# Attention and a two-layer feed-forward on one core: earlier due times for blocks a, b, d and VectorE's combinations in the second stage

## The chip, the cores and the metric

The kernel runs on one core of a Trainium2 chip. The time is the device time of one execution in microseconds (us); the time before is the median of three runs, 1447.98 us (1443.79 to 1448.81). The engines are called PE (matrix products; its weight loads are PEld), DVE (VectorE), ACT (ScalarE), POOL (GpSimd) and SP, which here only issues transfers.

## The reference

```python
def _attn_ref(q, k, v, g_q, g_k):            # (8, 12, 448, 64): 8 batches, 12 heads
    q_n, k_n = rmsnorm(q, g_q), rmsnorm(k, g_k)
    scores = (1 / np.sqrt(64)) * np.matmul(q_n, k_n.transpose(0, 1, 3, 2))
    attn = exp(scores - max);  attn = attn / (sum + 1e-9)
    return np.matmul(attn, v)

def _moe_ref(x, w_in, w_out):                # x: (3584, 768), w_in: (768, 2048), w_out: (2048, 768)
    h = x @ w_in
    g = h * np.cos(h)
    return g @ w_out
```

The attention's output, heads side by side, is `x`. All inputs and the output are float32.

## The kernel before, in words

The program has two stages, each with a planner of its own. The first stage does the attention of all 8 batches and the product with `w_in` for batches 0 to 6, and stores `h` in DRAM. It also makes seven combinations of quarters of `w_out` (the scheme that multiplies 2 by 2 blocks with seven products instead of eight) and stores them. The change touches the second stage alone.

The second stage begins with the product with `w_in` for batch 7 (16 blocks on PE), and then takes the batches in four pairs, 0 to 3. For each pair `h` is a matrix of 2 by 2 parts: two halves of the 2048 inner rows, two batches. The parts are called roles: a and c belong to the pair's first batch (first and second half), b and d to its second batch (likewise). Each role has four blocks, 0 to 3, of 2 x 128 rows by 448 columns, in tiles called B, so that `B1b3` is block 3 of role b of pair 1. The numbers in a profile are left out: there it is `B1b`.

A block is made so (`block`): SP loads it from DRAM (tile hb, L596); for each half ACT writes the rounded number of turns (n, L601), DVE subtracts the turns in two steps (L611 twice); ACT takes the absolute value (L615) and the sine (c, L619), and DVE multiplies c by hb (L623). There are three buffers for hb, and one each for n and c.

Seven products per pair follow on PE, called product 0 to 6. Their left operands are: a; b, after `b = d - b`; a, after `a = a + b`; c; b, after `b = d - a`; a, after `a = c - a`; and d. These combinations are written over the tiles block by block (L626). The first three run on DVE, in that order, and `a = c - a` on POOL. Before a block is multiplied, ACT casts it to a high part (ghi, L635) and POOL subtracts that from the block to get the low part (glo, L633). Both have three buffers. A product takes 4 blocks x 2 rows x 3 output columns x 3 matmuls (L648 high, L649 low, L650 with the weights' low part), 72 in all, 18 for each block. Results leave the six PSUM banks through ACT's copies (L673) and DVE's sums (L676), and go out through SP (L680). SP also loads the combined weights (wo, L279, eight buffers from product 2 on).

The order of the work on each engine is the planner's. Each piece has an engine, a cost, the pieces it depends on and a due time. The planner simulates the engines in time: whenever an engine is free, it takes, of the pieces that are ready by its own costs, the one that is due first. What comes out is one fixed list for each engine, and on the chip each engine runs its list in order, waiting where an operand is late. Due times so decide only what goes first among pieces that the planner holds ready; they delay nothing. A block's due time is given by its product's start in the planner's time (`D`), less `ahead`: the load is due 30 before that, the turns 20, the multiplication 12.

The tiles set limits of their own. Role a of the next pair takes over the tiles of c of this pair, d of the next pair those of a, and b those of b. So a block of the next pair can be begun only when the splits of its tile's last user are done.

Of the kernel before, what the change touches and what calls it, by code (L numbers as in the profile page):

```python
# [14 lines left out]
ALU = mybir.AluOpType  # L15
# [12 lines left out]
class Plan:  # L28
# [18 lines left out]
    def add(self, eng, cost, due, fn, *args, r=(), w=(), land=0.0, start=0.0, lead=None):  # L47
        n = len(self.parts)
        deps = set()
        for key in r:  # L50
            deps.update(self.writer.get(key, ()))
        for key in w:
            deps.update(self.writer.get(key, ()))
            deps.update(self.readers.get(key, ()))
        for key in (*r, *w):
            name, inst = key[0], key[1]
            if name in self.rings:
                self.users.setdefault((name, inst), []).append(n)
        for key in r:
            self.readers.setdefault(key, []).append(n)  # L60
        for key in w:
            self.writer[key] = [n]
            self.readers[key] = []
        deps.discard(n)
        self.parts.append((eng, cost, due, fn, args, deps, land))
        self.start.append(start)
        self.lead.append(self.LEAD * (eng == PE) if lead is None else lead)
# [59 lines left out]
def tile_attention_moe(  # L127
# [13 lines left out]
    B, S, D = 8, kT.shape[2], 64  # L141
# [101 lines left out]
    mix = {}  # L243
# [668 lines left out]
    for fc in range(NFC):  # L912
        d = BLOCK * fc
# [10 lines left out]
    def block(pr, role, g, d):  # L924
        i, j = ROLES[role]
        n = next(count)
        hb, B_ = ("hb", n), ("B", home(pr, role), g)
        r = [("hd", 2 * pr + j, NH * i + NG * g + f) for f in range(NG)]
        add(SP, ISS, d - 30.0, gl_load, pr, role, g, r=r, w=[hb], land=LAND)
        for f in range(NG):  # L930
            t = ("n", NG * n + f)
            add(ACT, 0.56, d - 20.0 + 1.5 * f, g_turns, pr, role, g, f, r=[hb], w=[t])
            add(DVE, 0.63, d - 19.0 + 1.5 * f, g_reduce, pr, role, g, f, 0, r=[hb, t], w=[B_])
            add(DVE, 0.63, d - 18.5 + 1.5 * f, g_reduce, pr, role, g, f, 1, r=[t], w=[B_])
        add(ACT, 0.96, d - 15.0, g_abs, pr, role, g, w=[B_])
        for f in range(NG):
            c = ("c", NG * n + f)
            add(ACT, 0.57, d - 13.0 + 1.5 * f, g_cos, pr, role, g, f, r=[B_], w=[c])
            add(DVE, 0.63, d - 12.0 + 1.5 * f, g_mul, pr, role, g, f, r=[hb, c], w=[(*B_, f)])

    def block_keys(pr, role, g):
        B_ = ("B", home(pr, role), g)
        return [B_] + [(*B_, f) for f in range(NG)]

    def mix(pr, to, a, c, op, d, eng=DVE):
        e, cost = (nc.vector, 1.2) if eng == DVE else (nc.gpsimd, 2.3)
        for g in range(NGR):
            add(eng, cost, d + BLOCK * g, g_mix, pr, to, a, c, g, op, e,
                r=sum((block_keys(pr, x, g) for x in (a, c) if x != to), []), w=block_keys(pr, to, g))

    def product(pr, pi, role):
        d0 = T0 + PROD * (NPR * pr + pi)
        for kk in range(NH // 2):
            if pi >= 2 or pr == 0:
                s = slot(pr, pi, kk)
                add(SP, ISS, d0 + BLOCK * kk - 24.0, v_place, pr, pi, kk, s, w=[("w", s)], land=8.0)
        for k in range(NH):
            d = d0 + PART * k
            g = k // NG
            if k % NG == 0:  # L960
                n = next(split_n)
                Bs, hi, lo = block_keys(pr, role, g), ("ghi", n), ("glo", n)
                add(ACT, 0.96, d - 8.0, g_split, pr, pi, role, g, 0, r=Bs, w=[hi])
                add(POOL, 2.3, d - 6.0, g_split, pr, pi, role, g, 1, r=Bs + [hi], w=[lo])
            s = slot(pr, pi, k // 2)
            add(PE, PART, d, ffn2, pr, pi, k, s, r=[hi, lo, ("w", s)], w=[("y", bank(pr, pi, oc)) for oc in range(NO)])
        return d0 + PROD

    def copies(pr, pi, name, d, where=None):
        for oc in range(NO):  # L970
            y = ("y", bank(pr, pi, oc))
            if where and pr == NPAIR - 1 and oc == NO - 1:
                add(ACT, 0.3, d + oc, e_copy, pr, pi, oc, name, 0, r=[y], w=[(name, oc)])
                add(DVE, 0.35, d + oc, e_copy, pr, pi, oc, name, 1, r=[y], w=[(name, oc, 1)])
            else:
                add(ACT, 0.53, d + oc, e_copy, pr, pi, oc, name, r=[y], w=[(name, oc)])
            if where:
                add(SP, ISS, d + oc + 1, e_store, pr, oc, name, *where, r=[(name, oc), (name, oc, 1)], land=LAND)

    def sums(pr, pi, to, a, d, where=None):  # L980
        for oc in range(NO):
            add(DVE, 0.63, d + oc, e_add, pr, pi, oc, to, a,
                r=[("y", bank(pr, pi, oc))] + ([(a, oc)] if a != to else []), w=[(to, oc)])
            if where:
                add(SP, ISS, d + oc + 1, e_store, pr, oc, to, *where, r=[(to, oc)], land=LAND)

    for pr in range(NPAIR):
        D = [T0 + PROD * (NPR * pr + pi) for pi in range(NPR + 1)]
        for roles, pi, ahead in (("a", 0, 12.0), ("bd", 1, 18.0), ("c", 3, 12.0)):
            for g in range(NGR):  # L990
                for n, role in enumerate(roles):
                    block(pr, role, g, D[pi] + BLOCK * g - ahead + 2 * n)
        d = product(pr, 0, "a")
        mix(pr, "b", "d", "b", ALU.subtract, D[1] - 12.0)
        copies(pr, 0, "e1", d + 1)
        mix(pr, "a", "b", "a", ALU.add, D[2] - 14.0)
        d = product(pr, 1, "b")
        copies(pr, 1, "e7", d + 1)
        d = product(pr, 2, "a")
        mix(pr, "b", "d", "a", ALU.subtract, D[3] - 10.0)  # L1000
        sums(pr, 2, "u3", "e7", d + 1)
        mix(pr, "a", "c", "a", ALU.subtract, D[3] - 2.0, POOL)
        d = product(pr, 3, "c")
        sums(pr, 3, "e1", "e1", d + 1, (0, 0))
        d = product(pr, 4, "b")
        sums(pr, 4, "c22", "e7", d + 1, (1, 1))
        d = product(pr, 5, "a")
        sums(pr, 5, "u3", "u3", d + 1, (1, 0))
        d = product(pr, 6, "d")
        copies(pr, 6, "c12", d + 1, (0, 1))  # L1010
# [52 lines left out]
```

## Time and profile before

| | before |
|---|---|
| median of three runs | 1447.98 us (1443.79 to 1448.81) |
| the profiled execution's own time | 1448.93 us |
| its span, first to last instruction | 1447.1 us |
| PE busy | 1397.0 us, 97% |
| PEld busy | 1152.7 us, 80% |
| DVE, ACT, POOL busy | 1020.8, 1001.6 and 932.6 us |
| mean granted PE clock | 0.998 |

Times inside a profile are counted from the span's start. In the answers that are quoted below, a row of a timeline has the start, the duration, the engine, the line, the operation, what is written and read, the number of instructions merged in it, and in brackets how long the engine sat idle before it and what ended that. A row of a table of stretches has the stretch, its length, the busy time and number of instructions of PE, PEld, DVE, ACT and POOL, the granted PE clock, the share of the DMA engines and the GB/s. Rows of waits have the total, the number of times and the longest.

### The profile page before, as it was taken

How to read it: one execution, taken by the hardware profiler on the slowest of the kernel's cores; microseconds unless marked ns; L12 is line 12 of the kernel's file. 1: busy time of each engine (PE TensorE's matmuls, PEld its weight loads, DVE VectorE, ACT ScalarE, POOL GpSimd, SP SyncE). 2: the span in 40 equal slices, each digit the busy share in tenths (PEclk: the TensorE clock that was granted, in tenths of full speed). 3: DMA queues.
4: the chain of work that ended last, by engine and by line, in shares of the span. 5: the costliest groups of instructions: out<-in, count | busy, mean ns of one | idle time of the engine just before them, and what ended most of it. 6: DMA issues, size and time to landing. Idle time of an engine off the chain costs nothing.

```text
span 1447.1 us, 22426 instructions
## 1 busy us (share of the span) xinstructions
PE 1397.0 (97%) x7361; PEld 1152.7 (80%) x7361; DVE 1020.8 (71%) x1649; ACT 1001.6 (69%) x2058; POOL 932.6 (64%) x722
## 2 busy tenths in 40 slices
PE   6999999999999999999999999999999999999998
PEld 2445687888888788787878788889889899899898
DVE  6878885677778777869676755536876876977821
ACT  5777677677777777777776676547676776786742
POOL 5678777566877867787884673101295596585684
PEclk9999999999999999999999999999999999999999
DMA  6788444555667576566654542149569569489373
GB/s 207 230 259 255 129 129 133 151 175 173 192 200 222 166 219 206 185 206 188 215 184 159 163 149 87 55 132 347 195 201 327 188 224 338 154 265 339 124 238 101
DMA packets 154452, 282.62 MB, mean 195 GB/s; under 512 B 31760, under 2 KB 102368, under 8 KB 154336
## 3 DMA queue, kind: packets, MB, share of 16 engines
q1 hardware_dynamic: 154336, 281.20, 60.7%
q8 instruction: 58, 0.95, 0.3%
q14 instruction: 58, 0.48, 0.1%
HBM read 218.24 MB, written 62.89 MB: 194 GB/s over the span
## 4 chain that ended last, share of the span: by engine, by line
PE 71%; DVE 14%; ACT 5%; DMA 4%; issue 4%; POOL 2%; SPq 0%; ACTq 0%; DVEq 0%; POOLq 0%
PE ph L573 9%; PE PT L483 8%; PE ph L574 8%; PE ph L575 8%; PE O L514 8%; PE S L438 7%; PE y L649 7%; PE y L650 7%; PE y L648 7%; DVE lo L502 2%; DMA hb<-h_d 2%; ACT hi L494 1%; POOL glo L633 1%; DVE sm L447 1%; PE O L522 1%
## 5 line engine op out<-in xcount | busy, mean ns | idle before, releaser
L573 PE MATMUL ph<-xs,wi 128*128 128x448 f32 x768 | 299.2, 390 | 1.5 <-ACT he L585 1.5
L574 PE MATMUL ph<-xs,wi 128*128 128x448 f32 x768 | 281.1, 366 | 0.0
L575 PE MATMUL ph<-xs,wi 128*128 128x448 f32 x768 | 281.0, 366 | 0.0
L456 ACT ACTIVATE P<-S,sm 128x448 f32<-128x448 f32 x336 | 213.7, 640 | 78.7 <-DVE sm L447 66.6
L649 PE MATMUL y<-glo,wo 128*128 128x448 f32 x672 | 247.1, 368 | 7.3 <-POOL glo L633 7.3
L648 PE MATMUL y<-ghi,wo 128*128 128x448 f32 x672 | 246.8, 367 | 0.3 <-ACT ghi L635 0.3
L650 PE MATMUL y<-ghi,wo 128*128 128x448 f32 x672 | 246.7, 367 | 0.0
L494 ACT CAST hi<-PT 128x448 fp32r<-128x448 f32 x312 | 153.5, 536 | 93.9 <-PE PT L483 49.6
L447 DVE TENSOR_REDUCE sm<-S 128x1 f32<-128x448 f32 x322 | 186.7, 611 | 25.6 <-PE S L438 24.9
L483 PEld LDWEIGHTS PT<-ident,P 128*128 128x128 f32 x1344 | 155.5, 141 | 41.6 <-issue 22.8
L502 DVE TENSOR_TENSOR lo<-PT,hi 128x448 fp32r<-128x448 f32 x234 | 134.7, 617 | 71.5 <-ACT hi L494 70.2
L483 PE MATMUL PT<-ident,P 128*128 128x128 f32 x1344 | 181.2, 275 | 3.0 <-DVE hi L492 3.0
L573 PEld LDWEIGHTS ph<-xs,wi 128*128 128x128 f32 x768 | 144.5, 188 | 34.9 <-issue 15.7
L575 PEld LDWEIGHTS ph<-xs,wi 128*128 128x128 f32 x768 | 144.2, 188 | 12.6
L574 PEld LDWEIGHTS ph<-xs,wi 128*128 128x128 f32 x768 | 144.9, 189 | 9.7 <-issue 0.4
L649 PEld LDWEIGHTS y<-glo,wo 128*128 128x128 f32 x672 | 126.6, 188 | 19.4 <-POOL glo L633 8.7
L306 POOL TENSOR_TENSOR r<-r,nhalf 128x14 f32<-128x14 f32 (+1 forms) x50 | 128.5, 2570 | 12.5 <-DVE r L324 8.9
L648 PEld LDWEIGHTS y<-ghi,wo 128*128 128x128 f32 x672 | 126.6, 188 | 11.7 <-ACT ghi L635 0.7
L650 PEld LDWEIGHTS y<-ghi,wo 128*128 128x128 f32 x672 | 126.6, 188 | 10.9
L438 PE MATMUL S<-khi,qhi 64*128 64x448 f32 x399 | 115.0, 518 | 1.7 <-ACT khi L343 1.2
L514 PE MATMUL O<-hi,vs 128*128 128x448 f32 x312 | 101.9, 381 | 7.3 <-ACT hi L494 3.3
L514 PE MATMUL O<-lo,vs 128*128 128x448 f32 x234 | 89.3, 397 | 10.3 <-DVE lo L502 9.8
(225 smaller groups left out, 2710.7 us busy)
## 6 DMA issues: line engine op xcount, KB each, us to landing
wo<-wo_d SPq DMA_DIRECT2D x88, 768.0 KB
h_d<-he SPq DMA_DIRECT2D x128, 224.0 KB
hb<-h_d SPq DMA_DIRECT2D x64, 448.0 KB
wo_d<-wv SPq DMA_DIRECT2D x56, 384.0 KB
sd<-sd SPq DMA_DIRECT2D x46, 448.0 KB
vd<-v SPq DMA_DIRECT2D x78, 160.0 KB
qd<-qT SPq DMA_DIRECT2D x48, 256.0 KB
raw<-w_in SPq DMA_DIRECT2D x16, 768.0 KB
```

Source lines behind the costliest of these rows:

```text
L438: nc.tensor.matmul(d["S", t][:, :S], d[a][p0:p1, j * 128 : j * 128 + 128], d[c][p0:p1, :], start=(n == 0), stop=(n == len(ops) - 1),)
L447: nc.vector.tensor_reduce(least, d["S", t][:, :S], axis=AX.X, op=ALU.min)
L456: nc.scalar.activation(tl(u, f"P{t}", [128, S], F32, "P"), d.pop(("S", t))[:, :S], AF.Exp, bias=sm[:, 1, t : t + 1], scale=-1.0, accum_out ...
L483: nc.tensor.transpose(pt[:, t * 128 : t * 128 + 128], src, ident)
L494: nc.scalar.copy(hi, pt[:, hh * S : hh * S + S])
L514: nc.tensor.matmul(O, st, d.pop((what, kb, hh)), start=(kc + n == 0), stop=(kc + n == 4))
L573: nc.tensor.matmul(ph[:, :S], whi, x2[:, 0, :], start=(cc == 0), stop=False)
L574: nc.tensor.matmul(ph[:, :S], whi, x2[:, 1, :], start=False, stop=False)
L575: nc.tensor.matmul(ph[:, :S], wlo, x2[:, 0, :], start=False, stop=(cc == NCC - 1))
L648: nc.tensor.matmul(y, whi, hi, start=(k == 0 and chain < 2), stop=False, skip_group_check=chain == 2)
L649: nc.tensor.matmul(y, whi, lo, start=False, stop=False, skip_group_check=chain == 2)
L650: nc.tensor.matmul(y, wlo, hi, start=False, stop=(k == NH - 1), skip_group_check=chain == 2)
```

## The change

Five due times of the second stage are set further ahead. The blocks of role a are due 30 instead of 12 ahead of their product, those of b and d 44 instead of 18; `b = d - b` 28 instead of 12, `a = a + b` 30 instead of 14, `b = d - a` 20 instead of 10. Block c, `a = c - a` on POOL, the splits, the products, the copies and sums and the weights' loads keep their due times. No instruction is added or removed; the compute engines run the same work in another order. On SP the same transfers are issued in another order too.

```diff
-        for roles, pi, ahead in (("a", 0, 12.0), ("bd", 1, 18.0), ("c", 3, 12.0)):
+        for roles, pi, ahead in (("a", 0, 30.0), ("bd", 1, 44.0), ("c", 3, 12.0)):
...
-        mix(pr, "b", "d", "b", ALU.subtract, D[1] - 12.0)
+        mix(pr, "b", "d", "b", ALU.subtract, D[1] - 28.0)
...
-        mix(pr, "a", "b", "a", ALU.add, D[2] - 14.0)
+        mix(pr, "a", "b", "a", ALU.add, D[2] - 30.0)
...
-        mix(pr, "b", "d", "a", ALU.subtract, D[3] - 10.0)
+        mix(pr, "b", "d", "a", ALU.subtract, D[3] - 20.0)
```

PE's list is the same in both kernels. On the other engines the lists differ at these three places.

First, DVE where product 1 of pair 0 needs its last block. `B0b3` and `B0a3` are block 3 of roles b and a of pair 0, `B0c0` is block 0 of role c. Before:

```order
L626 TENSOR_TENSOR B0b3_12013<-B0d3_12079,B0b3_12013 128x896
L611 SCALAR_TENSOR_TENSOR B0c0_12149<-n0c01_12157,hb0_4_12063 128x448
L611 SCALAR_TENSOR_TENSOR B0c0_12149<-n0c01_12157,B0c0_12149 128x448
L626 TENSOR_TENSOR B0a3_11624<-B0b3_12013,B0a3_11624 128x896
L626 TENSOR_TENSOR B0b2_11913<-B0d2_11972,B0a2_11558 128x896
```

Now:

```order
L626 TENSOR_TENSOR B0b3_12013<-B0d3_12079,B0b3_12013 128x896
L626 TENSOR_TENSOR B0a3_11624<-B0b3_12013,B0a3_11624 128x896
L611 SCALAR_TENSOR_TENSOR B0c0_12149<-n0c01_12157,hb0_4_12063 128x448
L611 SCALAR_TENSOR_TENSOR B0c0_12149<-n0c01_12157,B0c0_12149 128x448
L626 TENSOR_TENSOR B0b2_11913<-B0d2_11972,B0a2_11558 128x896
```

The combination of `B0a3` has moved ahead of two reductions of block c. It is the only move in pair 0 up to the end of product 2.

Second, DVE at the same place of pair 1 (pair 2 is alike). Rows of L626 that write a tile of b from d and a are `b = d - a`, for product 4. Before:

```order
L626 TENSOR_TENSOR B1b0_12627<-B1d0_12682,B1a0_12386 128x896
L626 TENSOR_TENSOR B1b1_12738<-B1d1_12843,B1a1_12457 128x896
L623 TENSOR_TENSOR B1d3_13091<-c1d30_13145,hb3_7_13022 128x448
L611 SCALAR_TENSOR_TENSOR B1c0_13163<-n1c00_13147,hb2_4_13075 128x448
L611 SCALAR_TENSOR_TENSOR B1c0_13163<-n1c00_13147,B1c0_13163 128x448
L623 TENSOR_TENSOR B1d3_13091<-c1d31_13165,hb3_7_13022 128x448
L626 TENSOR_TENSOR B1b3_13036<-B1d3_13091,B1b3_13036 128x896
```

Now:

```order
L626 TENSOR_TENSOR B1b3_12981<-B1d3_13042,B1b3_12981 128x896
L626 TENSOR_TENSOR B1a3_12573<-B1b3_12981,B1a3_12573 128x896
L611 SCALAR_TENSOR_TENSOR B1c0_13099<-n1c01_13116,hb2_4_13027 128x448
L611 SCALAR_TENSOR_TENSOR B1c0_13099<-n1c01_13116,B1c0_13099 128x448
L626 TENSOR_TENSOR B1b0_12627<-B1d0_12681,B1a0_12386 128x896
L611 SCALAR_TENSOR_TENSOR B1c1_13168<-n1c10_13165,hb2_5_13092 128x448
L611 SCALAR_TENSOR_TENSOR B1c1_13168<-n1c10_13165,B1c1_13168 128x448
L626 TENSOR_TENSOR B1b1_12741<-B1d1_12800,B1a1_12457 128x896
L626 TENSOR_TENSOR B1b2_12856<-B1d2_12915,B1a2_12498 128x896
```

The two combinations for product 4 that stood ahead of `B1b3` stand behind it now, among the reductions of block c. Two more reductions (`B1c1`, second half), the first multiplication of `B1c0`, the combination that writes `B1b3` for product 4 and two reductions of `B1c2` follow, and then the second multiplication of `B1c0`. In pair 3 only one of the two combinations has moved behind, and the second multiplication of `B3c0` comes four rows sooner than that.

Third, POOL at the turn from product 1 to product 2 of pair 1 (`glo1pk` is the low part of block k for product p). Before:

```order
L633 TENSOR_TENSOR glo113_13199<-B1b3_13036,ghi113_13193 128x896
L633 TENSOR_TENSOR glo120_13214<-B1a0_12386,ghi120_13196 128x896
L633 TENSOR_TENSOR glo121_13247<-B1a1_12457,ghi121_13229 128x896
L626 TENSOR_TENSOR B1a0_12386<-B1c0_13163,B1a0_12386 128x896
L633 TENSOR_TENSOR glo122_13286<-B1a2_12498,ghi122_13260 128x896
```

Now:

```order
L633 TENSOR_TENSOR glo113_13187<-B1b3_12981,ghi113_13183 128x896
L633 TENSOR_TENSOR glo120_13218<-B1a0_12386,ghi120_13212 128x896
L626 TENSOR_TENSOR B1a0_12386<-B1c0_13099,B1a0_12386 128x896
L633 TENSOR_TENSOR glo121_13267<-B1a1_12457,ghi121_13247 128x896
L633 TENSOR_TENSOR glo122_13287<-B1a2_12498,ghi122_13280 128x896
```

POOL's combination `a = c - a` of block 0, which reads `B1c0`, now stands ahead of the split of block 1 for product 2. It is so in pairs 1, 2 and 3, not in pair 0. On SP the last load of b and d of a pair (`hb3_7` in pair 1) has moved from behind the weights `wo1_3_3` and three stores to just behind `wo1_3_2`; in pair 3 it has only passed the three stores.

## The prediction

> **What bounds the kernel now.** I read the page first, then PE's waits in the second stage, then the timelines of the engines that PE waits for.
>
> ```profile
> span 1447.1 us, 22426 instructions
> PE 1397.0 (97%) x7361; PEld 1152.7 (80%) x7361; DVE 1020.8 (71%) x1649; ACT 1001.6 (69%) x2058; POOL 932.6 (64%) x722
> ```
>
> PE is busy for 97% of the span, and the change gives it no instruction less. So only PE's waits can be won, and only those of the second stage. From 962 us to the end these are all:
>
> ```profile
> PE y L649 <- POOL glo L633: 7.3, 4, 2.6
> PE y L648 <- ACT ghi L635: 0.3, 1, 0.3
> ```
>
> Four waits for a low part, one in each pair, and a short one for a high part. In PE's timeline they are (the first three rows are pair 0's, the next three pair 1's):
>
> ```profile
> 1047.36 0.37 PE L650 MATMUL y<-ghi,wo 128*128 128x448 f32 x1
> 1048.08 0.47 PE L648 MATMUL y<-ghi,wo 128*128 128x448 f32 x1 [0.35 <-ACT ghi L635]
> 1051.16 0.47 PE L649 MATMUL y<-glo,wo 128*128 128x448 f32 x1 [2.61 <-POOL glo L633]
> ...
> 1156.73 0.37 PE L648 MATMUL y<-ghi,wo 128*128 128x448 f32 x1
> 1158.50 0.47 PE L649 MATMUL y<-glo,wo 128*128 128x448 f32 x1 [1.41 <-POOL glo L633]
> 1158.81 0.37 PE L650 MATMUL y<-ghi,wo 128*128 128x448 f32 x1
> ...
> 1262.54 0.47 PE L649 MATMUL y<-glo,wo 128*128 128x448 f32 x1 [1.62 <-POOL glo L633]
> ...
> 1366.58 0.48 PE L649 MATMUL y<-glo,wo 128*128 128x448 f32 x1 [1.63 <-POOL glo L633]
> ```
>
> Each stands at the second matmul of block 3 of product 1: `b = d - b` is late there. The first cost more than its wait, as the table of stretches shows:
>
> ```profile
> 1051.67:1055.08 3.41, 3.41 (x11) 3.05 (x10) 3.38 (x6) 1.22 (x3) 3.41 (x2) 0.50 0.00 0
> 1158.50:1162.05 3.55, 3.55 (x17) 3.30 (x18) 3.52 (x5) 1.73 (x3) 3.55 (x2) 1.00 0.00 0
> ...
> 1115.88:1130.76 14.88, 14.88 (x74) 13.51 (x73) 10.85 (x18) 9.16 (x13) 8.00 (x5) 1.00 0.96 318
> 1191.30:1205.90 14.60, 14.60 (x74) 13.53 (x73) 9.78 (x18) 10.96 (x17) 8.07 (x4) 1.00 0.96 332
> ```
>
> After 2.61 us of idling PE was granted half its clock for 3.41 us, which loses 1.7 us; after 1.41 us (second row) nothing was taken. The last two rows show a second thing: the same work, 74 matmuls begun, takes 14.88 us before the wait at 1158.50 (in the ninth of the 28 products) and 14.60 after it. I see no cause for this spacing that the change touches, so it enters the range only.
>
> **Term 1, pair 0.** Here DVE and POOL meet:
>
> ```profile
> 1045.88 1.09 DVE L626 TENSOR_TENSOR B0b<-B0d,B0b 128x896 f32<-128x896 f32 x1
> ...
> 1048.09 1.08 DVE L626 TENSOR_TENSOR B0a<-B0b,B0a 128x896 f32<-128x896 f32 x1
> 1049.09 2.97 DVE L626 TENSOR_TENSOR B0b<-B0d,B0a 128x896 f32<-128x896 f32 x1
> ```
>
> ```profile
> 1048.10 3.00 POOL L633 TENSOR_TENSOR glo<-B0b,ghi 128x896 fp32r<-128x896 f32 x1 [5.46 <-ACT ghi L635]
> ...
> 1146.85 2.13 POOL L633 TENSOR_TENSOR glo<-B1b,ghi 128x896 fp32r<-128x896 f32 x1 [1.59 <-ACT ghi L635]
> 1155.44 3.00 POOL L633 TENSOR_TENSOR glo<-B1b,ghi 128x896 fp32r<-128x896 f32 x1 [6.47 <-ACT ghi L635]
> 1158.41 5.92 POOL L633 TENSOR_TENSOR glo<-B1a,ghi 128x896 fp32r<-128x896 f32 x2
> 1164.29 2.14 POOL L626 TENSOR_TENSOR B1a<-B1c,B1a 128x896 f32<-128x896 f32 x1
> ```
>
> A split takes 2.13 us alone, but 3.00 when DVE began a combination 0.01 us before it; the next combination then takes 2.97 instead of 1.09. One waits until the other is through. In pair 0 the combination of `B0b3` (1045.88) keeps its place, so the block itself comes no sooner. But the one of `B0a3` now follows it directly and is over at about 1048.1, when the split starts. The split ends some 0.8 us sooner, PE idles 1.8 instead of 2.6. Of the idle times shown, 1.41 to 1.63 left the clock alone (the later products ran at 14.60) and 2.61 did not; 1.8 is nearest to the former, so I count the 1.7 too. **Term 1: -2.5 us**, bounds 0 (the split is held after all) and -2.5. The rest of that wait stays.
>
> The Trainium skill ("TensorE: Matmul & The Clock Gate", "Why this matters for your kernels") asks for no idle gaps over about 3 us, as one idle window brings the half clock; here 2.61 us did, so the measurement decides. By that figure 1.8 us would be safe, and the sum the same.
>
> **Term 2, the old wait in pairs 1 to 3.** From 1156.73 to 1158.50 and 1158.81 PE made two steps in 2.08 us that take 0.41 at the spacing around them: 1.67 lost. With the idle times 1.62 and 1.63 in place of 1.41 the other two are 1.9 each: 5.5 together. What makes `B1b3` late:
>
> ```profile
> 1147.31 3.61 DVE L626 TENSOR_TENSOR B1b<-B1d,B1a 128x896 f32<-128x896 f32 x2
> 1150.85 0.61 DVE L623 TENSOR_TENSOR B1d<-c1d,hb 128x448 f32<-128x448 f32 x1
> ...
> 1153.22 1.09 DVE L626 TENSOR_TENSOR B1b<-B1d,B1b 128x896 f32<-128x896 f32 x1
> 1154.22 0.62 DVE L611 SCALAR_TENSOR_TENSOR B1c<-n1c,hb 128x448 f32<-128x448 int32 x1
> ...
> 1155.42 1.08 DVE L626 TENSOR_TENSOR B1a<-B1b,B1a 128x896 f32<-128x896 f32 x1
> 1156.42 2.98 DVE L626 TENSOR_TENSOR B1b<-B1d,B1a 128x896 f32<-128x896 f32 x1
> ...
> 1161.04 1.30 DVE L626 TENSOR_TENSOR B1b<-B1d,B1a 128x896 f32<-128x896 f32 x1
> ...
> 1163.45 0.61 DVE L623 TENSOR_TENSOR B1c<-c1c,hb 128x448 f32<-128x448 f32 x1
> ```
>
> ```profile
> 1123.44 4.08 SPq L279 DMA_DIRECT2D wo<-wo_d  x2
> 1127.61 0.42 SPq L596 DMA_DIRECT2D hb<-h_d  x1
> 1130.88 0.36 SPq L279 DMA_DIRECT2D wo<-wo_d  x1
> 1133.38 1.32 SPq L680 DMA_DIRECT2D out<-es  x3
> 1134.82 29.63 SPq L596 DMA_DIRECT2D hb<-h_d  x5
> ```
>
> Two combinations for product 4 held DVE for 3.61 us ahead of it; they have moved behind. And its last load went out at 1134.82, behind a weight at 1130.88 that waits for PE and three stores. It now stands behind the weight that goes out at about 1127.2 (the second of the merged row at 1123.44), so it can leave at 1127.7, 7.1 us sooner, in pairs 1 and 2; in pair 3, where it passes the stores only, at 1131.3, 3.5 sooner. The combination of b3 then starts between 1149.6 (3.6 sooner, by DVE's list alone) and some 1145.4 (load and list together, as far as ACT and POOL let it). I carry the load's gain through: 1146.1 in pairs 1 and 2, 1149.7 in pair 3. (I count pair 3 in pair 1's times.) The split must be done by 1156.9, where PE would go on without a wait (one place of 0.2 after 1156.73), and in between lie the combination (1.09), a cast of 0.95 and a split of 2.13 to 3.00: 2 us are to spare in pair 3 and more in the others. Only ACT's new list, which has some turns and an absolute value of block c ahead of that cast, can leave a rest: 0 to 0.8, taken as 0.2 each. **Term 2: -4.9 us**, bounds -5.5 and -3.1.
>
> **Term 3, a new wait.** On POOL `a = c - a` of block 0 now stands ahead of the split of block 1 for product 2, and so that split, which PE wants, is queued behind DVE's second multiplication of `B1c0` (1163.45 before). PE wants it two blocks after the second matmul of product 1's block 3, at 1156.9 + 2 x 3.72 (a quarter of 14.88) = 1164.4. From the combination of b3 to that multiplication DVE's new list has 6 combinations at 1.0 (1153.22 to 1154.22), 8 reductions at 0.6 (two from 1154.22 to 1155.42) and 2 multiplications at 0.6: 12.0 us. Meanwhile POOL has four splits, and combinations wait for them: in the same stretch of before, with as many of both, the rows 3.61, 1.09, 1.08, 2.98 and 1.30 are 4.1 us over six times 1.0. So `B1c0` is done at 1146.1 + 12.0 + 4.1 = 1162.2, the combination (2.14) and the split (2.13) take until 1166.5, and PE waits **2.1 us in pairs 1 and 2**. In pair 3 there are 4 combinations, 6 reductions and 2 multiplications, 8.8 us, and two thirds of the waiting, 2.7: 1149.7 + 8.8 + 2.7 + 4.3 = 1165.5, **1.1 us**. At 2.1 PE idles about 1.9, and the clock stays as in term 1. **Term 3: +5.3 us**; bounds: 0, if the combinations meet no split (1146.1 + 12.0 + 4.3 = 1162.4, in time), and 2.3 more in each pair, with a half clock's 1.7, if three whole splits are waited for (6.4 instead of 4.1; the fourth runs beside reductions). I take the value that before's own rows give.
>
> The Trainium skill ("SBUF — State Buffer", "SBUF: two separate sides") calls the pair of ports that DVE and GpSimd share an exclusive lock, held for a whole instruction; the rows 3.00 and 2.97 agree. As an estimate from that rule at its worst, four splits of 2.13 cost DVE 8.5 us instead of 4.1, the new waits would be 4 to 6.5 us, and the sum about +15.
>
> What else moves costs nothing by the cover it has: the blocks of the next pair stand earlier in ACT's list among the casts of products 5, 6 and 0, but casts wait for PE to free a buffer:
>
> ```profile
> ACT ghi L635 <- PE y L650: 71.6, 55, 2.7
> ```
>
> Such a cast (0.95) and split (2.13) end 3.1 us after the buffer is free, and PE wants them two blocks, 7.4 us, after that: 4 us of cover. Without it each microsecond more would show as a wait for glo at product 0. DVE's sums (L676) of product 5 stand a few rows later; their bank is wanted only a product later.
>
> **Sum:** 1448.9 (the profiled execution's own time) - 2.5 - 4.9 + 5.3 = **1446.8**. That execution lies 0.9 above the median of the runs, within their spread, so I leave it so.
>
> **Rivals.** *No new wait.* If block c is done in time, the whole old wait is won: 1448.9 - 2.5 - 5.5 = 1440.9. For it speaks that blocks c could start sooner too; against it, that `B1c0` has to be done at 1160.1, 4.0 sooner than in before, though two more reductions and two more combinations stand between it and `B1b3`.
>
> *Slower: the new wait is long.* POOL's combination holds back the split in three pairs by 4.4, 4.4 and 3.4 us (the upper bound of term 3), each over 2.61, so each takes the half clock: 12.2 + 5.1 - 2.5 - 4.9 = +9.9, 1458.8. It decides from an idle time of 2.6 us, 0.7 over my value. For it: the combinations of DVE stand closer together than before and each can meet a split.
>
> *The order changes and the time does not.* Loads are held by three buffers and by SP's list; if they land no sooner and the rest of block b3 stays as it is, only term 1's 0.8 remains: 1448.
>
> **How the numbers follow.** The forecast has 0.57, no new wait 0.22, the long wait 0.15, nothing 0.06. The forecast's own range is 1442 to 1451: the new waits between 0.5 and 3 us, and the spacing, which alone is worth +5.3 (19 of 28 products at 14.88 instead of 14.60) or -2.5 (9 the other way). About 0.5%, 7.2 us, is what a measurement of this kernel can tell from no change: under 1440.7 or over 1455.2. Faster is half of the first rival and a tenth of the forecast, 0.17, put at 0.18; slower two thirds of the second and little of the forecast, 0.13; the rest, 0.69, the same. Until 2 in 10 are out, the range goes from 1439.5 to 1455.5.
>
> **What will show it.** Right: in PE's waits of the second stage `glo` at the last block of product 1 is short in pairs 1 to 3, and waits of 1 to 3 us stand at the second block of product 2, released by POOL, whose row before it is a combination released by a multiplication of c (L623) on DVE; pair 0's wait falls from 2.61 to 1.8 with no half clock behind it. Wrong: term 2, if product 1 still waits over 1 us; term 3, if POOL's combination starts before 1160 in the old count and PE runs through product 2. Waits at product 0 or 6 would mean that the cover of the casts was used up.

## The result, and the profile after

The changed kernel takes 1459.23 us (median of four runs, 1458.39 to 1463.37), the kernel before 1448.08. The ratio is 1.0095, 95% interval 1.0074 to 1.0116: about 11 us slower, outside the predicted range and on the other side of it.

The profiled execution, from the page of the changed kernel:

```profile
span 1456.4 us, 22440 instructions
PE 1402.9 (96%) x7361; PEld 1156.7 (79%) x7361; DVE 1034.1 (71%) x1649; ACT 1000.5 (69%) x2058; POOL 930.4 (64%) x722
```

The span grew by 9.3 us. PE is busy for 5.9 us longer with the same instructions, so part of that is a lower clock. PE's waits of the second stage, from 962 us to the end:

```profile
PE y L649 <- POOL glo L633: 9.8, 7, 2.4
PE y L648 <- ACT ghi L635: 2.2, 3, 1.3
```

Before there were 7.3 and 0.3. In PE's timeline the waits are these (the first three rows are pair 1's, the next four pair 2's, the last two pair 3's; one of 0.28 at block 1 of product 1 in pair 1 is left out):

```profile
1153.00 0.47 PE L648 MATMUL y<-ghi,wo 128*128 128x448 f32 x1 [0.42 <-ACT ghi L635]
1155.42 0.47 PE L649 MATMUL y<-glo,wo 128*128 128x448 f32 x1 [1.94 <-POOL glo L633]
1165.36 0.47 PE L649 MATMUL y<-glo,wo 128*128 128x448 f32 x1 [0.83 <-POOL glo L633]
...
1260.83 0.47 PE L648 MATMUL y<-ghi,wo 128*128 128x448 f32 x1 [0.43 <-ACT ghi L635]
1263.24 0.47 PE L649 MATMUL y<-glo,wo 128*128 128x448 f32 x1 [1.95 <-POOL glo L633]
...
1273.16 0.47 PE L649 MATMUL y<-glo,wo 128*128 128x448 f32 x1 [2.36 <-POOL glo L633]
...
1277.45 0.47 PE L649 MATMUL y<-glo,wo 128*128 128x448 f32 x1 [0.38 <-POOL glo L633]
...
1379.19 0.47 PE L648 MATMUL y<-ghi,wo 128*128 128x448 f32 x1 [1.32 <-ACT ghi L635]
1381.73 0.74 PE L649 MATMUL y<-glo,wo 128*128 128x448 f32 x1 [2.06 <-POOL glo L633]
```

In pair 0 no wait is listed any more. In pairs 1 and 2 the wait at block 3 of product 1 is still there and longer, with one for the high part ahead of it. New are waits at blocks 1 and 2 of product 2. The lengths of the products, from the starts of their first matmuls in PE's timeline (us):

| | product 1 before | after | product 2 before | after |
|---|---|---|---|---|
| pair 1 | 16.49 | 19.59 | 14.59 | 15.68 |
| pair 2 | 16.49 | 17.62 | 14.59 | 17.99 |
| pair 3 | 16.50 | 14.88 | 14.59 | 19.97 |

Some of these stretches in the table of stretches (PE, PEld, DVE, ACT, POOL, then the granted clock):

```profile
1140.93:1160.52 19.59, 16.95 (x73) 14.67 (x72) 19.28 (x20) 10.61 (x18) 10.31 (x4) 0.91 0.14 45
1156.21:1159.62 3.41, 3.41 (x11) 3.02 (x10) 3.38 (x6) 2.04 (x3) 2.07 (x1) 0.50 0.00 0
...
1249.17:1266.79 17.62, 15.24 (x74) 13.36 (x73) 17.34 (x17) 9.63 (x16) 10.33 (x4) 1.00 0.14 49
...
1374.05:1394.02 19.97, 16.59 (x73) 14.66 (x72) 12.98 (x21) 13.77 (x21) 17.10 (x8) 0.91 0.45 140
```

The clock of 0.91 is a half clock of 3.41 us inside the stretch, which costs 1.7; pair 1 has one in product 1 (second row) and pair 3 one in product 2. DVE is the engine that has no slack in product 1: it is busy for 19.28 of 19.59 us (what an instruction waits for POOL inside its own duration counts as busy), while POOL, which PE waits for, works 10.31.

The whole account of the 9.3 us: product 2 of pair 0 begins 2.9 sooner (1053.38 instead of 1056.29, although PE began product 0 1.8 later, behind a first stage that is not touched), product 1 of pairs 1 to 3 costs 2.6 more (+3.1, +1.1, -1.6), product 2 of these pairs 9.9 more (+1.1, +3.4, +5.4), and the two spacings of the matmuls (14.59 or 14.88 us for a product) come out 0.3 in favour.

**What is late in pair 1.** The change moves rows in ACT's list too, beside the three places shown ahead of the prediction, and this is where the loss begins. Before, ACT made the cast of `B1b3` for product 1 as soon as the block was done, ahead of the turns of `B1c1` and the absolute value of `B1c0`:

```profile
1154.42 0.95 ACT L635 CAST ghi<-B1b 128x896 fp32r<-128x896 f32 x1 [1.19 <-DVE B1b L626]
...
1156.11 0.54 ACT L601 ACTIVATE n1c<-hb 128x448 int32<-128x448 f32 x1
1156.59 0.94 ACT L615 ACTIVATE B1c<-B1c 128x896 f32<-128x896 f32 x1
```

DVE after the change, the combinations from `B1b3` on, and the second multiplication of `B1c0`:

```profile
1143.18 2.94 DVE L626 TENSOR_TENSOR B1b<-B1d,B1b 128x896 f32<-128x896 f32 x1
1146.22 2.82 DVE L626 TENSOR_TENSOR B1a<-B1b,B1a 128x896 f32<-128x896 f32 x1
...
1152.34 3.97 DVE L626 TENSOR_TENSOR B1b<-B1d,B1a 128x896 f32<-128x896 f32 x2
...
1160.34 0.61 DVE L623 TENSOR_TENSOR B1c<-c1c,hb 128x448 f32<-128x448 f32 x1
```

ACT at the same place, where the cast now stands behind those two rows:

```profile
1144.18 0.94 ACT L673 COPY e<-y 128x448 f32<-128x448 f32 x2
1150.27 0.55 ACT L601 ACTIVATE n1c<-hb 128x448 int32<-128x448 f32 x1 [5.14 <-DVE B1c L611]
1150.75 0.94 ACT L615 ACTIVATE B1c<-B1c 128x896 f32<-128x896 f32 x1
1151.60 0.52 ACT L673 COPY e<-y 128x448 f32<-128x448 f32 x1
1152.01 0.94 ACT L635 CAST ghi<-B1b 128x896 fp32r<-128x896 f32 x1
```

POOL:

```profile
1143.04 5.05 POOL L633 TENSOR_TENSOR glo<-B1b,ghi 128x896 fp32r<-128x896 f32 x2 [3.13 <-ACT ghi L635]
1153.02 2.34 POOL L633 TENSOR_TENSOR glo<-B1b,ghi 128x896 fp32r<-128x896 f32 x1 [4.93 <-ACT ghi L635]
...
1161.09 2.14 POOL L626 TENSOR_TENSOR B1a<-B1c,B1a 128x896 f32<-128x896 f32 x1 [2.82 <-DVE B1c L623]
1163.18 4.21 POOL L633 TENSOR_TENSOR glo<-B1a,ghi 128x896 fp32r<-128x896 f32 x2
```

Read together: the combination of `B1b3` starts 0.14 us behind a split and takes 2.94 instead of 1.09, the one of `B1a3` meets the next split and takes 2.82. `B1b3` is done at 1146.1, but its cast stands in ACT's list behind the turns of `B1c1`, which need the one buffer n. That comes free only with DVE's reductions of `B1c0`, behind both combinations. ACT sits idle for 5.14 us with the cast that PE wants three rows further back. The cast begins 5.9 us after its block is done. Then block c is late in the same way, POOL idles 2.82 for it, and the split for product 2 ends at 1165.4, where PE has waited since 1164.5.

How much DVE's combinations of pair 1 waited can be read from the groups of instructions (of each four, busy in total, mean ns of one). Before:

```profile
L626 DVE TENSOR_TENSOR B1b<-B1d,B1a 128x896 f32<-128x896 f32 x4 | 7.9, 1992 | 0.0
L626 DVE TENSOR_TENSOR B1b<-B1d,B1b 128x896 f32<-128x896 f32 x4 | 5.2, 1301 | 0.1
L626 DVE TENSOR_TENSOR B1a<-B1b,B1a 128x896 f32<-128x896 f32 x4 | 4.8, 1202 | 0.9 <-POOL glo L633 0.9
```

After:

```profile
L626 DVE TENSOR_TENSOR B1b<-B1d,B1b 128x896 f32<-128x896 f32 x4 | 10.4, 2588 | 0.1
L626 DVE TENSOR_TENSOR B1a<-B1b,B1a 128x896 f32<-128x896 f32 x4 | 8.5, 2123 | 0.1
L626 DVE TENSOR_TENSOR B1b<-B1d,B1a 128x896 f32<-128x896 f32 x4 | 6.3, 1602 | 0.0
```

Twelve combinations took 17.9 us before and 25.2 after. Undisturbed they take 13.0 (12 x 1.08).

### The profile page after: what moved, and what is told of

Read it like the earlier page. It is cut to its first block, busy times and chain, and to the rows that moved or that the text cites. A ratio compares the mean times of both kernels' runs of the same rounds, so it can differ in the third digit from the quotient of the medians.

```text
span 1456.4 us, 22440 instructions
## 1 busy us (share of the span) xinstructions
PE 1402.9 (96%) x7361; PEld 1156.7 (79%) x7361; DVE 1034.1 (71%) x1649; ACT 1000.5 (69%) x2058; POOL 930.4 (64%) x722
## 4 chain that ended last, share of the span: by engine, by line
PE 63%; DVE 18%; ACT 6%; DMA 5%; issue 4%; POOL 2%; SPq 1%; ACTq 0%; DVEq 0%; POOLq 0%
PE ph L573 9%; PE PT L483 9%; PE ph L574 8%; PE ph L575 8%; PE O L514 8%; PE S L438 8%; DMA hb<-h_d 4%; PE y L649 4%; PE y L650 4%; PE y L648 4%; PE O L522 2%; DVE lo L502 1%; ACT hi L494 1%; DVE sm L447 1%; DVE B2b L626 1%
## 5 line engine op out<-in xcount | busy, mean ns | idle before, releaser
L514 PE MATMUL O<-lo,vs 128*128 128x448 f32 x234 | 88.9, 395 | 10.7 <-DVE lo L502 10.4
```

What stands on the lines that cost most here:

```text
L514: nc.tensor.matmul(O, st, d.pop((what, kb, hh)), start=(kc + n == 0), stop=(kc + n == 4))
```

## The experiments

After the trace there were three explanations. **A**: the due times of b and d make lists in which casts and splits stand behind the work of block c, on ACT and POOL. **B**: the combinations that are due earlier stand closer together and meet POOL's splits; a meeting is a combination on DVE and an instruction on POOL of which one waits for the other. **L**: whatever the lists, all the waits come from these meetings. All ratios are to the kernel before, run beside the experiment; that of the change itself is 1.0095 (1.0074 to 1.0116).

| run | what | median us | ratio (95% interval) |
|---|---|---|---|
| e1_bd_only | only b and d due 44 ahead | 1460.65 | 1.0091 (1.0070 to 1.0113) |
| e2_bd_back | the change, b and d back to 18 | 1441.76 | 0.9964 (0.9948 to 0.9981) |
| e3_free_after | the change, combinations meet nothing | 1437.21 | 0.9929 (0.9911 to 0.9947) |
| e4_free_before | before, combinations meet nothing | 1440.32 | 0.9948 (0.9928 to 0.9969) |
| e5_plan_knows | the change, planner knows the meetings | 1443.31 | 0.9954 (0.9932 to 0.9976) |
| e6_before_knows | before, planner knows the meetings | 1456.51 | 1.0055 (1.0030 to 1.0079) |
| e7_cast_first | the change, one cast moved on ACT | 1457.14 | 1.0052 (1.0030 to 1.0075) |
| e8_free_mix4 | the change, product 4's combinations free | 1447.47 | 0.9987 (0.9967 to 1.0008) |
| e9_pool_later | the change, one combination moved on POOL | 1455.39 | 1.0048 (1.0031 to 1.0066) |
| e10_mixa_only | only `a = a + b` due 30 ahead | 1443.81 | 0.9969 (0.9949 to 0.9989) |
| e11_cut_matmul | e5 with one matmul cut in two per pair | 1439.37 | 0.9935 (0.9915 to 0.9956) |

**Which of the five edits.** e1_bd_only makes one edit alone:

```diff
-        for roles, pi, ahead in (("a", 0, 12.0), ("bd", 1, 18.0), ("c", 3, 12.0)):
+        for roles, pi, ahead in (("a", 0, 12.0), ("bd", 1, 44.0), ("c", 3, 12.0)):
```

> Of the five edits only the due times of blocks b and d (44 instead of 18) are made. Theory A: this edit alone makes the loss. With b and d early, the planner lets ACT's turns of block c (one buffer n) stand ahead of the casts of products 1 and 2, and the chip's DVE comes to them later than the planner's. The changed kernel lost 12.5 us in products 1 and 2 of pairs 1 to 3 and won 2.9 in pair 0. Here pair 0 is as before, so up to +12: 1453 to 1461 us, waits at product 2 in every pair from 1 on. Rival B: the combinations that are due earlier (28, 30, 20) make the loss, since they stand closer together and meet POOL's splits. Then this kernel is no slower than before: 1442 to 1449.

e2_bd_back takes that edit back and keeps the other four:

```diff
-        for roles, pi, ahead in (("a", 0, 30.0), ("bd", 1, 44.0), ("c", 3, 12.0)):
+        for roles, pi, ahead in (("a", 0, 30.0), ("bd", 1, 18.0), ("c", 3, 12.0)):
```

> The changed kernel with the due times of blocks b and d put back to 18; the other four edits stay. Theory A: the loss goes, the gain of pair 0 (2.9 us) stays, and in pairs 1 to 3 the combination of a's block 3 stands directly behind that of b's, out of the way of the split, which gains about 0.8 us in each: 1448 - 2.9 - 2.4 = 1442.7, range 1437 to 1446; no waits over 0.5 us at product 2. Rival B: the combinations are still due early, so the loss stays: 1455 to 1460.

e10_mixa_only makes only the edit of `a = a + b` (`D[2] - 30.0` instead of `D[2] - 14.0`).

> Of the five edits only that of a = a + b (30 instead of 14). In DVE's list the combination of a's block 3 stands directly behind that of b's block 3 in every pair, and so is over when the split of b's block 3 starts. Term 1 of the prediction: the split takes 2.13 instead of 3.00, so the four waits at product 1 are 0.8 shorter each, and the first one's half clock (1.7) goes: 1448.5 - 3.2 - 1.7 = 1443.6, range 1440 to 1446. If the split is held all the same, or what is behind becomes late: 1447 to 1450.

e1 is 12 us slower than the kernel before, with waits of 1.9 and 2.9 us at product 2 in pair 1, 3.3 in pair 2 and 0.6 and 2.1 in pair 3. e2 and e10 are faster than before. So it is b and d's due times that lose, and B as the edit to blame is out. With the other four edits (e2) the kernel is 0.4% faster than before. PE's waits in e2 (second stage):

```profile
PE y L649 <- POOL glo L633: 2.5, 4, 0.7
```

In e10 product 1 of pairs 1 to 3 takes 15.66, 15.60 and 15.66 instead of 16.5, so 0.8 to 0.9 less in each, as term 1 said. In pair 0 its split of block 3 ends at 1050.44 instead of 1051.10, but there PE had come 1.0 sooner, idled 1.68 and 1.69, and took the half clock all the same: product 1 is 20.24 long. This execution took 1448.92, one of the longest of its twelve; that the median lies near the expected 1443.6 is in part luck.

**Take the meetings away.** In e3_free_after and e4_free_before each combination on DVE reads zeros from PSUM (64 columns of the bank of c that nothing uses) in place of its second block. The subtraction or addition of that block is left out; the count of elements and the lists stay:

```diff
+    FREE = (("b", "d", "b"), ("a", "b", "a"), ("b", "d", "a"))
...
+        if eng is nc.vector and (to, a, c) in FREE:
+            t, x = (blk[(pr, k, g)].rearrange("p f (q s) -> p (f q) s", s=64) for k in (to, a))
+            eng.tensor_tensor(t, x, ys["c"][:, S:].unsqueeze(1).broadcast_to([128, 14, 64]), op)
+            return
         eng.tensor_tensor(blk[(pr, to, g)], blk[(pr, a, g)], blk[(pr, c, g)], op)
```

> The changed kernel, but each combination on DVE (L626) takes zeros from PSUM in place of its second block (the subtraction or addition of that block is left out), so that it has one operand in SBUF and should not meet POOL. Lists are those of the changed kernel. Theory L: all waits of PE in the second stage come from DVE and POOL waiting for each other. The combinations then take about 1.0 us each always, splits 2.1, and PE runs through: the waits at products 1 and 2 (17.8 us beyond the spacing, half clocks included) go: 1459 - 17.8 = 1441, and 1437 if all 28 products run at 14.6; equal to the next kernel within 4 us. Rival A: the lists alone make the waits (turns and casts on ACT, the combination ahead of the split on POOL): at least half of the 12.5 us remain, 1450 or more, and over 5 us more than the next kernel.

> The kernel before with the same replacement in its combinations on DVE. Theory L: its four waits (10.4 us beyond the spacing with the half clock) go as well: 1448 - 10.4 = 1437.6, range 1434 to 1442, the same as the changed kernel without the meetings. Rival A: its waits are those of its list, of which two combinations for product 4 ahead of block 3 of role b are the main part: only some 3 us go, 1443 to 1447.

The groups of e3 (the eight combinations on DVE that write role b of pair 1, and the twelve splits of its role a on POOL):

```profile
L632 DVE TENSOR_TENSOR B1b<-B1d,c 128x896 f32<-128x896 f32 x8 | 8.6, 1083 | 0.1
...
L641 POOL TENSOR_TENSOR glo<-B1a,ghi 128x896 fp32r<-128x896 f32 x12 | 25.5, 2133 | 16.2 <-ACT ghi L643 16.2
```

With one operand in PSUM these combinations take 1083 ns in the mean, and none of the 48 over 1091; a split takes 2133. In the second stage of e3 PE waits for nothing at all, though ACT, POOL and DVE run the very lists that lost 11 us (DVE has one instruction more, which writes the zeros). e4 still waits 3.6 us in five places. So L holds for the changed kernel. For the kernel before it holds in part: PE's idle time falls from 7.6 to 3.6 us, and what is left does not come from these meetings. The new lists are, without meetings, even a little better than the old ones, and the loss of the change is what the meetings make of them. (Without its read of a, a combination for product 4 no longer holds back POOL's `a = c - a`; but that waits for a multiplication of c which stands later in DVE's list anyway.) The Trainium skill ("SBUF — State Buffer", "SBUF: two separate sides") says that DVE and GpSimd exclude each other there when the DVE instruction has two inputs in SBUF; 1083 ns in e3 against means of up to 2588 in the changed kernel agrees.

e8_free_mix4 frees only the combinations for product 4 (`FREE = (("b", "d", "a"),)`; of those the subtraction of a is left out):

> The changed kernel, with only the combinations for product 4 (b = d - a) taking zeros from PSUM in place of a (that subtraction is left out), so that they meet nothing; those for products 1 and 2 still do. If the meetings of product 4's combinations, which stand among the reductions of block c, hold the path: the waits at product 2 (9.9 us in three pairs) go, those at product 1 stay: about 1449. If it is the two combinations for products 1 and 2 (2.94 and 2.82 us), nearly all waits stay: 1456 to 1460.

It came out at 1447.5. Product 2 takes 15.38, 14.96 and 14.67 (after the change: 15.68, 17.99, 19.97); product 1 still takes 16.75 and 18.93 in pairs 1 and 2. So most of the waits at product 2 come from the meetings of the combinations for product 4 that stand among the reductions of block c. Those at product 1 stay here and are gone in e3, so they need the meetings of `b = d - b` and `a = a + b`.

**Move one instruction.** e7_cast_first changes ACT's list alone, in pairs 1 and 2; DVE's order stays:

```diff
+    for pr in (1, 2):
+        i = order.index((g_turns, (pr, "c", 1, 0)))
+        j = order.index((g_split, (pr, 1, "b", 3, 0)))
+        late = [x for x in order[i:j] if x[0] in (g_turns, g_abs, g_reduce, g_mix)]
+        order[i : j + 1] = [x for x in order[i : j + 1] if x not in late] + late
```

> The changed kernel with one move in ACT's list, in pairs 1 and 2: the copy and the cast of b's block 3 for product 1 go ahead of the turns and the absolute value of block c that stood ahead of them. Theory A: those turns, which sit idle 5.1 us for DVE, are why product 1 waits there: its waits in pairs 1 and 2 go (5.0 and 3.0 us beyond the spacing, one half clock in it). The block that product 2 wants comes no sooner by this, so a part turns into a longer wait there: a net of 0 to 8 us less, I take 4: 1455, and no wait at product 1 of these pairs. If instead the meetings with POOL make block 3 late (2.94 us for its combination), the wait at product 1 stays above 1.5 us.

Product 1 now takes 14.88 and 15.16 in these pairs, so the cast behind the turns was what held it; that this place was late at all is the meetings' doing (e3). But product 2 takes 20.19 and 20.87: in both pairs together the two products need 71.1 us, with the change they needed 70.9. In the profiled execution all that was won at product 1 was given back one product later, since block c came no sooner; what it shows less is product 2 of pair 3 (17.71 instead of 19.97), where nothing was moved. By their ratios e7 is 0.4% below the change, with intervals that just touch, so a small gain of the move is neither shown nor excluded.

e9_pool_later changes POOL's list alone, in pairs 1 to 3 (`order.insert(j, order.pop(i))`, with i the combination `a = c - a` of block 0 and j the split of block 1 for product 2):

> The changed kernel with one move in POOL's list, in pairs 1 to 3: a = c - a of block 0 goes behind the split of block 1 for product 2. Term 3 of the prediction says that the wait at product 2 is this combination's place. In the profile after, the cast for that split is over at 1161.9, 1268.2 and 1379.1 us (pairs 1 to 3), so a split of 2.1 could be through at 1164.0, 1270.4 and 1381.3, where it was at 1165.4, 1273.1 and 1381.7: 1.2, 2.7 and 0.4 us won at most, with the half clock of pair 3 perhaps 6 in all: 1453 to 1456. If term 3 were the whole of it, all 9.9 us beyond the spacing at product 2 would go: 1449. The rival from the meetings says that the wait is handed on to the next block, since blocks c and casts are late themselves: 1456 or more.

e9 is 0.5% faster than the change by the ratios, and its median lies in the expected range of 1453 to 1456. But in the profile product 2 takes 15.47, 18.81 and 18.38, only 1.0 less in the sum; 2.1 less is product 1 of pair 2 (15.50), where nothing was moved. POOL in pair 2 of e9, and the wait that PE then had:

```profile
1264.44 2.13 POOL L633 TENSOR_TENSOR glo<-B2a,ghi 128x896 fp32r<-128x896 f32 x1 [2.20 <-ACT ghi L635]
1266.54 4.22 POOL L626 TENSOR_TENSOR B2a<-B2c,B2a 128x896 f32<-128x896 f32 x2
1270.72 4.17 POOL L633 TENSOR_TENSOR glo<-B2a,ghi 128x896 fp32r<-128x896 f32 x2
```

```profile
1272.86 0.48 PE L649 MATMUL y<-glo,wo 128*128 128x448 f32 x1 [2.28 <-POOL glo L633]
```

The split of block 1 ends in time (1266.57), and PE waits 2.28 at block 2 instead, whose split stands behind two of those combinations. So a place in a list was mended, and the lateness went to the next place.

**Let the planner know.** If the lists are fine but for the meetings, it should help to have the planner reckon with them. e5_plan_knows is the changed kernel with

```diff
+            if e == POOL or fn in self.both:
+                o = DVE if e == POOL else POOL
+                t = max(t, self.held[o])
+                self.held[e] = t + cost
```

in the planner's loop (`both` holds `g_mix` in the second stage, and nothing in the first); e6_before_knows is the same with the due times of before.

> The changed kernel's due times, with a second-stage planner that knows the meeting: a combination on DVE and any piece on POOL begin in its time only when the other is through. Theory P: the due times of the change are sound, and what is wrong is that the planner places combinations at once where they wait 1 to 3 us on the chip, so that its lists put work of block c on ACT and POOL ahead of casts and splits that PE wants. With the meetings in its time the lists should fit the chip: waits of at most about 1 us in each pair, the sum near that of the kernel without meetings (1437) and some 2 us above: 1436 to 1443. Rival A': due times of 44 for b and d put turns ahead of casts whatever the planner knows of POOL: the waits at product 2 stay, 1453 or more.

> The due times of the kernel before, with the planner that knows the meeting. Theory P alone (knowing the meeting is all that matters) would have it win as much as the kernel above, 1438 to 1443. If early due times are needed too (theory P+), combinations that are due 12 ahead still stand behind other work, their waits count once more in the planner's own time, and nothing is won: waits of 1 to 3 us at product 1 in each pair, 1444 to 1453.

e5 is faster than before, by 0.5%, and 1.1% faster than the change with the same due times (by the medians, from two sets of runs); it missed its range by 0.3 us. PE's waits in its second stage:

```profile
PE y L654 <- POOL glo L638: 0.3, 1, 0.3
```

So A' is out: with the meetings in the planner's time, 44 and 30 do no harm. The meetings are still there: the 48 combinations keep DVE busy for 74.1 us in e5, for 73.7 before, 88.4 with the change and 51.8 in e3. In e5 they stand where PE does not wait for them. e6 missed the range that I gave it and is slower than before: product 1 of pairs 1 to 3 takes 20.77, 21.31 and 19.22, with waits like 1.45 for the high part and 2.62 for the low part in pair 1. Knowing the meetings is not enough; with combinations due only 12 ahead the planner puts that of `B1b3` later still, 10.4 us after the start of product 1 instead of 7.7. So the due times of 44 for b and d need the planner that knows, and that planner needs early due times. But the pair of them is not the only way: e2, with the old planner and without the 44, gained as much as e5 within the intervals (0.9964 and 0.9954).

e5 has next to no waits left, yet from its first product to the end it takes 419.8 us, where e3 took 414.8. Its products run at the longer spacing: 22 of 28 take 14.88, five 14.59. (The expectation below counts 24 and 26; with 22 the most to win is 22 x 0.29 = 6.4 us.) e11_cut_matmul cuts one matmul of e5 into two of 224 columns in each pair:

```diff
-            nc.tensor.matmul(y, wlo, hi, start=False, stop=(k == NH - 1), skip_group_check=chain == 2)
+            parts = [slice(0, S)] if (pi, k, oc) != (0, 1, 0) else [slice(0, S // 2), slice(S // 2, S)]
+            for x in parts:
+                nc.tensor.matmul(
+                    y[:, x], wlo, hi[:, x], start=False, stop=(k == NH - 1), skip_group_check=chain == 2
+                )
```

> The due times of the change with the planner that knows the meeting, as in the run of 1443.3 us, in which PE waited 0.3 us in all but ran 24 of its 28 products at 14.88 us. Here one matmul of product 1 (first row, first output column, the weights' low part) is cut into two of 224 columns in each pair, and nothing else. Spacing theory: a break in the even row of matmuls can switch PE from 206.7 to 202.7 ns, as breaks of 0.3 to 1.8 us did in the profiles; if this one does in pair 0, 26 products at 14.6 gain up to 26 x 0.29 = 7.5 us less the time of the extra instruction (0.1 us each): 1436 to 1439. If a break has to be a wait, or the switch is by chance, no change: 1440 to 1445.

The expectation names the place wrongly; as the diff shows, it is the second row of product 0. PE's timeline around the cut in pair 0, and two stretches, of e5 and then of e11:

```profile
1024.71 0.37 PE L654 MATMUL y<-glo,wo 128*128 128x448 f32 x1
1024.92 0.38 PE L657 MATMUL y<-ghi,wo 128*128 128x224 f32 x2
1025.13 0.37 PE L653 MATMUL y<-ghi,wo 128*128 128x448 f32 x1
1025.34 0.36 PE L654 MATMUL y<-glo,wo 128*128 128x448 f32 x1
1025.54 0.36 PE L657 MATMUL y<-ghi,wo 128*128 128x448 f32 x1
1025.73 0.37 PE L653 MATMUL y<-ghi,wo 128*128 128x448 f32 x1
```

```profile
1122.63:1137.51 14.88, 14.88 (x73) 13.52 (x72) 13.90 (x18) 12.48 (x20) 10.61 (x5) 1.00 0.62 204
```

```profile
1051.91:1066.50 14.59, 14.59 (x73) 13.52 (x72) 12.58 (x19) 13.24 (x21) 11.78 (x6) 1.00 0.60 201
```

From the cut on the matmuls follow each other every 0.203 us instead of 0.207, and stay so to the end. PE has no wait in the whole second stage; from the first product to the end it takes 412.9 us, 6.8 less than in e5's profile. That is one execution of each. The medians of 1439.4 and 1443.3 us come from two sets of runs. Their intervals against before, 0.9915 to 0.9956 and 0.9932 to 0.9976, overlap, so the gain in the time itself is probable and not sure. Against the kernel before the gain is sure: among the kernels that compute everything e11 has the lowest median, by its ratio 0.65% below the kernel before, and by the medians 1.4% below the change.

## Why the prediction was wrong

*What bounds the kernel* held: PE's waits in the second stage, the half clocks behind them and the spacing make the account, but for the 1.8 us by which PE began later.

*Term 1* (-2.5) came out at -2.9 for pair 0. The step itself (the combination of a's block 3 out of the way of the split, 0.8) is confirmed by e10's 0.8 to 0.9 in pairs 1 to 3. The 1.7 for the half clock was not earned by that step: in e10 the half clock came in spite of it. After the change the wait was small because PE started product 1 there 1.8 us later, while DVE's blocks came when they came (`B0b3` at 1045.41, before at 1045.88). That the term met its size is in part luck.

*Term 2* (-4.9) is the first step that failed: measured +2.6. It counted on the combination of `B1b3` taking 1.09, and took "0 to 0.8" as all that ACT's new list could leave. The combination took 2.94 and the cast came 5.9 us after it. I had seen that turns and an absolute value of block c stand ahead of the cast, and allowed less for them than their own durations (0.55 and 0.94), and nothing for what they wait for: the buffer n, free only when DVE is through two combinations and two reductions. In pair 3, where the cast does stand ahead of the turns, the wait went as predicted (14.88).

*Term 3* (+5.3) had the place and, in pairs 1 and 2, the releaser right, and the size wrong: +9.9. The step is the 4.1 us for meetings from `b`'s block 3 to `B1c0`. In pair 1 the six combinations of that stretch took 2.94, 2.82, 1.08, 3.97 (two) and 1.27, 6.1 over six times 1.0, near the upper bound of 6.4. With the combination starting 1.7 later after the start of product 1 than I had it (2.25 instead of 0.53), `B1c0` was done 20.0 us after that start, and not 16.6. I took the number of before's rows over as if it belonged to the work. It belongs to the order: e3 has the same work and none of it. Over half of the 9.9 is pair 3's: there the combination of `B3b3` started as forecast (4.4 after the start of product 1; I had 4.1), but the four combinations of the stretch took 4.6 over four times 1.0 and not 2.7. The cast of the split that I had queued behind POOL's combination was itself late, until 1379.1, behind turns that waited 3.08 us for DVE; PE idled 1.32 for it and 2.06 for the split, and a half clock followed. e9 shows that POOL's combination was also not one wait that could be taken out, since the next block is held by the next combinations.

*The rivals.* The long wait was priced at 1458.8 with a chance of 0.15, and the time came out there, though not by its sum: the new waits cost 9.9 and not 12.2 and 5.1 for clocks, and the old wait, which it took as won, grew instead. So its price came near by luck, but its condition, combinations that meet splits, is what happened. The estimate from the Trainium skill's lock ("SBUF — State Buffer", "SBUF: two separate sides") at its worst, +15, was nearer to the measured +11 than the forecast; of its 8.5 us of meetings 6.1 were measured in pair 1.

*The clock.* I held 1.8 us of idling for safe. In pair 1 idle times of 0.42 and 1.94 with one matmul between them were followed by a half clock, while 0.43 and 1.95 in pair 2, and 2.36 alone, were not. In e9 one of 1.95 in product 1 of pair 1 was (0.55 granted over the next 3.47 us). How long PE idles does not decide it alone; what does stays open.

*The cover.* No wait for product 0 or 6 appeared, as forecast.

## What to carry to other kernels

Two engines that shut each other out make a cost of the order, not of the instructions. A planner that does not know of it fills what it takes for free time with work that then stands ahead of what the bottleneck wants, and earlier due times give it more such time; here all five together won only with a planner that knew the exclusion (e5), and without it the four that leave b and d alone won as much (e2). When a row moves ahead of one that matters, price it by when its operands and its buffer are there and not by its duration; and when one place is mended, look which place is late next before counting the gain.

## What the runs showed of the hardware

Matmuls of the same form run at one of two even spacings, 206.7 or 202.7 ns (14.88 or 14.59 us for a product of 72), with nothing waited for and the granted clock at 1.00 in both. The spacing changes at breaks of the row: in the kernel before at the wait of 1.41 us in pair 1; in the changed kernel to the shorter one in pair 0 and back to the longer one at the wait at 1277.45. One cut matmul changed it at once in the profile of e11. The break can be small: in e3 it was 0.09 us, in product 0 of pair 1. What decides to which side a break goes is open. In a stage of 28 products it is worth up to 8 us (28 x 0.29), nearly as much as the change lost.

A combination of 128 x 896 elements on DVE took 1083 ns with its second operand in PSUM (64 columns read over and over), the same as undisturbed with both in SBUF (1.08 to 1.09 us), and was never held up by POOL in e3: none of the 48 took over 1091 ns.
